# The sum of row and output bias: from GpSimd's queue to a late place in VectorE's

## The chip, the cores and the metric

One core of a Trainium2 chip runs the whole program in one launch. The metric is the device time of an execution in microseconds (us), as a median of several runs. One execution is also recorded by the hardware profiler; all rows below come from that one, and their times count from the start of its span.

## The reference

A row is one of 2048 tokens, 448 wide, bf16. Four blocks follow each other: a spectral block, an FFN, and the same two again, with the same weights each time.

```
x = x + A(layernorm(x))     # A: 2-D real FFT, times (w_r + i w_i), inverse FFT
x = x + B(layernorm(x))     # B: relu(x @ w1 + b1)^2 @ w2 + b2, inner width 1792
x = x + A(layernorm(x))
x = x + B(layernorm(x))
```

The layer norm has no gain and no bias. The change touches only the FFN's residual: `x + b2` is needed when the result of the second matrix product is added.

## The kernel before, in words

The 2048 rows lie in `x_sb` as 16 row tiles t of 128 rows by 448. The FFTs are matrix products with constant matrices. The inverse transform ends in `stage_TI(t)` and `stage_AI(t)`, for two row tiles at a time ("a pair"): TensorE multiplies, ScalarE copies the first product out of PSUM, TensorE multiplies again, and VectorE adds the second product into `x_sb`. That add is the first VectorE instruction of the FFN for that pair (form `x_sb<-ps,x_sb 128x896`).

Then the pair's layer norm. `ln_B1(t)` makes the statistics (L548 and L549 on VectorE, a square root on ScalarE) and the sum of the change: `xb = x_sb + b2row`, 128x896, on GpSimd. `ln_B2(t)` makes the reciprocal (L556) and `nmr` (L559) on VectorE, then normalizes the even tile on ScalarE and the odd tile on VectorE (L485) into `y2`; GpSimd copies a pad of 64 columns for each of the two (L480), and SyncE issues a transposing DMA into `yT`.

The FFN runs in four chunks of four row tiles. `h_part(c, fb)` is four matmuls of 512 columns, a Relu out of PSUM on ScalarE and a square on VectorE into `hbuf`, 14 times for each chunk. `o_tile(t)` is 14 matmuls of 448 columns, and VectorE adds `xb[:, t]` to their sum and writes `x_sb` again. `xb` lies in the same arena as the inverse transform's input Z, so it can be written only when Z has been read. After the first FFN, `second_A(t)` starts the next spectral block row tile by row tile; after the second, the row tile is stored.

The order of the instructions on each engine is worked out by a planner ahead of the launch, which simulates the engines with assumed costs. A unit is one instruction, or all matmuls into one PSUM tile. Its priority is the longest path to the end plus a bias that is set by hand; in the FFN the bias falls by 5500 for each row tile. Each engine takes, among the units whose inputs are there, the one that can start first, and the priority decides between equals:

```
            u.prio = tail + sum(op.cost for op in u.ops) + u.ops[-1].lat
            u.prio += u.bias
                    start = max(r, free[e])
                    key = (start, -u.prio, u.seq)
```

On the chip, each engine then runs its list strictly in that order, and waits on semaphores for what the other engines and the DMAs bring. The assumed cost of the sum is set in the helper `tt`: `rate = 0.96 if isinstance(a, _PsAP) or eng == "pool" else 1.92`, and `cost=_free(o) / rate + 65.0` nanoseconds. All operations recorded by `tt` carry line L476, all matmuls L454, all ScalarE operations L472.

Of the kernel before, what the change touches and what calls it, by code (L numbers as in the profile page):

```python
# [6 lines left out]
ALU = mybir.AluOpType  # L7
# [3 lines left out]
P = 128  # L11
S = 2048
D = 448
# [141 lines left out]
def _res(a):  # L155
    return a.ap() if isinstance(a, _PsAP) else a
# [210 lines left out]
def _free(ap):  # L367
    n = 1
    for step, cnt in list(ap.ap)[1:]:
        n *= cnt  # L370
    return n


def bass_interleave_layers__spectral_gfnet__dense_activation_squared_relu__prompt_kernel(nc, A_x, A_w_r, A_w_i, B_x, B_w1, B_b1, B_w2, B_b2, out):
# [4 lines left out]
    sch = _Sched()  # L379

    with ExitStack() as es:
        onchip = set()

        def sb(name, shape, dt=BF16):
            t = es.enter_context(nc.sbuf_tensor(name, shape, dt))
            onchip.add(t.name)
            return t

        x_sb = sb("x_sb", [P, NT, D])
# [6 lines left out]
        xb = arena[:, 2 * FB * 512:2 * FB * 512 + NT * D].rearrange("p (t d) -> p t d", t=NT)  # L396
# [23 lines left out]
        b2row = sb("b2row", [P, D])  # L420
# [53 lines left out]
        def tt(o, a, b, op, eng="dve"):  # L474
            rate = 0.96 if isinstance(a, _PsAP) or eng == "pool" else 1.92
            sch.add(eng, lambda e: e.tensor_tensor(o, _res(a), b, op), [a, b], [o], cost=_free(o) / rate + 65.0)  # L476
# [69 lines left out]
        def ln_stats(ts_):  # L546
            for t in ts_:
                small(lambda e, t=t: e.bn_stats(st[:, t, 0:6], x_sb[:, t, :]), [x_sb[:, t, :]], [st[:, t, 0:6]], 530.0)  # L548
                small(lambda e, t=t: e.bn_aggr(mv[:, t, 0:2], st[:, t, 0:6]), [st[:, t, 0:6]], [mv[:, t, 0:2]])  # L549
            a, b = ts_[0], ts_[-1] + 1  # L550
            act(rstd[:, a:b, 0], mv[:, a:b, 1], ACT.Sqrt, bias=epst[:, 0:1])
# [158 lines left out]

        def ln_B1(t):
            ln_stats([t, t + 1])
            tt(xb[:, t:t + 2, :], x_sb[:, t:t + 2, :], b2row[:, None, :].to_broadcast([P, 2, D]), ALU.add, eng="pool")

        def ln_B2(t):
            ln_rstd([t, t + 1], True)
# [48 lines left out]
        def ffn(last):  # L765
            for t in range(0, NT, 2):
                sch.bias = 5500.0 * (NT - t)
                stage_TI(t)
                stage_AI(t)
                ln_B1(t)  # L770
                ln_B2(t)
            for c in range(4):
                sch.bias = 22000.0 * (4 - c)
                for fb in range(FB):
                    h_part(c, fb)
                for t in range(4 * c, 4 * c + 4):
                    sch.bias = 5500.0 * (NT - t)
                    o_tile(t)
                    if last:
                        dma("sp", out_dram[:, t, :], x_sb[:, t, :])  # L780
                    else:
                        ln_stats([t])
                        ln_rstd([t], False)
                        second_A(t)
# [90 lines left out]
```

## Time and profile before

| | |
|---|---|
| time, median of 3 runs | 338.5 us (338.15 to 339.89) |
| the profiled execution | 338.62 us, span 336.8 us |
| TensorE clock, mean granted | 0.965 of full |
| busy share of the span: PE, DVE, ACT, POOL | 85%, 61%, 53%, 17% |

PE is TensorE, PEld its weight load, DVE is VectorE, ACT is ScalarE, POOL is GpSimd. [...] The span begins with the first instruction and ends with the last; the remaining 1.8 us of the execution lie around it. In a row of the chain of waits, the time is that for which the chain stayed with this instruction; in a row of the timeline it is the instruction's own duration, and what stands in square brackets is how long its engine had been idle, and what ended that.

### The profile page before, as it was taken

The numbers are of one execution on the slowest core, as the hardware profiler recorded it, in microseconds if no ns is written. First come the engines' busy times: TensorE is split into PE (matmuls) and PEld (weight loads), VectorE is DVE, ScalarE is ACT, GpSimd is POOL, SyncE is SP. The second block draws the span as 40 slices with busy tenths as digits, with TensorE's granted clock in tenths as the row PEclk, the third lists the DMA queues.
The fourth block names the chain that finished last, engine by engine and source line by source line (L and its number), as shares of the span: only waits on it lengthen the run. The fifth ranks groups of instructions, "written<-read, shape, count | busy, mean of one in ns | idle before, by whom it ended". The sixth has DMA issues, their size and how long they took to land.

```text
span 336.8 us, 4428 instructions
## 1 busy us (share of the span) xinstructions
PE 285.0 (85%) x1574; PEld 154.8 (46%) x1574; DVE 205.1 (61%) x499; ACT 178.5 (53%) x293; POOL 56.3 (17%) x81
## 2 busy tenths in 40 slices
PE   0979857857799999899996975774799999999996
PEld 0656534533354454455454652443344445445442
DVE  5705992799867555776455499159973342463432
ACT  2669955655634706645813885555573271451730
POOL 4991000454300000200000000045530000010000
PEclk9999977999999999999999898799789999999999
DMA  7994000033210000010000000002231100002001
GB/s 300 409 371 75 1 2 0 0 69 70 50 34 0 0 2 0 0 34 1 0 2 0 0 2 0 0 0 65 63 79 31 41 0 29 27 0 74 14 14 41
DMA packets 25621, 16.00 MB, mean 48 GB/s; under 512 B 19392, under 2 KB 24000, under 8 KB 25600
## 3 DMA queue, kind: packets, MB, share of 16 engines
q1 hardware_dynamic: 25312, 15.43, 15.0%
q10 hardware_dynamic: 288, 0.30, 0.3%
q8 instruction: 12, 0.20, 0.2%
q14 instruction: 9, 0.07, 0.1%
HBM read 9.70 MB, written 1.84 MB: 34 GB/s over the span
## 4 chain that ended last, share of the span: by engine, by line
PE 64%; DVE 24%; ACT 5%; issue 2%; POOL 2%; DMA 1%; DVEq 0%; POOLq 0%; ACTq 0%
PE ps L454 64%; DVE tmp L476 7%; DVE x_sb L476 4%; DVE st L548 4%; DVE arena L476 3%; DVE tmp L485 2%; ACT arena L472 2%; DVE nmr L559 2%; ACT XA L472 2%; DMA x_sb<-in_A_x_dram 1%; ACT VT L472 1%; POOL Fs L485 1%; DVE mv L549 1%; POOL Ms L485 1%; DVE rstd L556 0%
## 5 line engine op out<-in xcount | busy, mean ns | idle before, releaser
L454 PE MATMUL ps<-yT,W_sb 128*128 128x512 bf16 x448 | 101.7, 387 | 5.6 <-ACT arena L472 5.6
L472 ACT ACTIVATE arena<-ps,b1f 128x512 bf16<-128x512 f32 x112 | 75.3, 685 | 47.0 <-PE ps L454 47.0
L454 PE MATMUL ps<-W_sb,arena 128*128 128x448 bf16 x448 | 86.9, 352 | 0.0
L476 DVE TENSOR_TENSOR arena<-arena 128x512 bf16<-128x512 bf16 x112 | 49.6, 443 | 40.0 <-ACT arena L472 39.9
L454 PEld LDWEIGHTS ps<-yT,W_sb 128*128 128x128 bf16 x448 | 44.2, 99 | 61.2 <-ACT arena L472 8.1
L476 POOL TENSOR_TENSOR arena<-x_sb,b2row 128x896 bf16<-128x896 bf16 x16 | 30.3, 1907 | 215.7 <-DVE x_sb L476 179.5
L454 PEld LDWEIGHTS ps<-W_sb,arena 128*128 128x128 bf16 x448 | 43.8, 98 | 40.1
L472 ACT ACTIVATE XA<-ps 128x512 bf16<-128x512 f32 (+1 forms) x48 | 32.5, 701 | 28.1 <-PE ps L454 27.7
L476 DVE TENSOR_TENSOR x_sb<-ps,arena 128x448 bf16<-128x448 f32 x32 | 19.9, 623 | 37.0 <-PE ps L454 37.0
L548 DVE BATCH_NORM_STATS2 st<-x_sb 128x6 f32<-128x448 bf16 x64 | 38.4, 614 | 3.0 <-DMA x_sb<-in_A_x_dram 2.4
L454 PE MATMUL ps<-H_sb,arena 128*128 128x256 bf16 x128 | 22.9, 330 | 11.3 <-DVE arena L476 9.9
L472 ACT ACTIVATE arena<-ps 128x904 bf16<-128x904 f32 x32 | 28.0, 931 | 5.9 <-PE ps L454 5.6
L472 ACT ACTIVATE rstd<-mv,epst 128x2 f32<-128x2 f32 (+1 forms) x40 | 11.7, 293 | 35.5 <-DVE mv L549 35.4
L476 DVE TENSOR_TENSOR x_sb<-ps,x_sb 128x896 bf16<-128x896 f32 x16 | 16.8, 1071 | 18.6 <-PE ps L454 18.6
L472 ACT ACTIVATE VT<-ps 128x512 bf16<-128x512 f32 (+1 forms) x36 | 18.6, 551 | 13.9 <-PE ps L454 13.6
L454 PEld LDWEIGHTS ps<-H_sb,arena 128*128 128x128 bf16 x128 | 13.5, 115 | 20.5 <-DVE arena L476 14.3
L454 PE MATMUL ps<-XA,FI_sb 128*128 128x448 bf16 x64 | 14.1, 354 | 9.5 <-ACT XA L472 9.5
L485 DVE TENSOR_SCALAR tmp<-x_sb,mv,rstd 128x224 bf16<-128x224 bf16 (+1 forms) x48 | 20.3, 453 | 1.4
L472 ACT ACTIVATE tmp<-x_sb,nmr,rstd 128x448 bf16<-128x448 bf16 x16 | 12.2, 759 | 13.1 <-DVE nmr L559 12.9
L476 DVE TENSOR_TENSOR tmp<-arena 128x904 bf16<-128x904 bf16 (+1 forms) x16 | 8.9, 567 | 16.2 <-ACT arena L472 16.1
L454 PE MATMUL ps<-Fs,x_sb 128*128 128x256 bf16 x32 | 9.8, 324 | 10.0 <-POOL Fs L485 9.1
L454 PE MATMUL ps<-arena,G_sb 128*128 128x452 bf16 (+1 forms) x72 | 15.1, 342 | 3.3 <-ACT arena L472 2.0
(40 smaller groups left out, 208.3 us busy)
## 6 DMA issues: line engine op xcount, KB each, us to landing
x_sb<-in_A_x_dram SPq DMA_DIRECT2D x4, 448.0 KB, 5.3
out_dram<-x_sb SPq DMA_DIRECT2D x16, 112.0 KB, 1.7
W_sb<-in_B_w_dram SPq DMA_DIRECT2D x1, 1568.0 KB, 19.7
W_sb<-in_B_w_dram SPq DMA_DIRECT2D x1, 1344.0 KB, 15.1
yT<-in_A_w_r_dram SPq DMA_DIRECT2D x1, 900.0 KB, 9.1
yT<-in_A_w_i_dram SPq DMA_DIRECT2D x1, 900.0 KB, 10.9
H_sb<-c_H SPq DMA_DIRECT2D x1, 896.0 KB, 12.1
G_sb<-c_G SPq DMA_DIRECT2D x1, 672.0 KB, 7.4
```

Source lines behind the costliest of these rows:

```text
L454: sch.add("pe", lambda e: e.matmul(_res(o), lhsT, rhs, start=start, stop=stop, skip_group_check=skip), [lhsT, rhs], [o], cost=max(_free(rh ...
L472: sch.add("act", lambda e: e.activation(o, _res(i), func, **kw), rd, [o], cost=c)
L476: sch.add(eng, lambda e: e.tensor_tensor(o, _res(a), b, op), [a, b], [o], cost=_free(o) / rate + 65.0)
L485: sch.add(eng, lambda e: e.tensor_scalar(o, i, s1, s2, op0=op0, **kw), rd, [o], cost=_free(o) / (1.4 if eng == "pool" else 1.92) + 65.0)
L548: small(lambda e, t=t: e.bn_stats(st[:, t, 0:6], x_sb[:, t, :]), [x_sb[:, t, :]], [st[:, t, 0:6]], 530.0)
L549: small(lambda e, t=t: e.bn_aggr(mv[:, t, 0:2], st[:, t, 0:6]), [st[:, t, 0:6]], [mv[:, t, 0:2]])
L559: small(lambda e: e.scalar_tensor_tensor(out=n, in0=m, scalar=-1.0, in1=r, op0=ALU.mult, op1=ALU.mult), [m, r], [n])
```

## The change

The sum is no longer put in GpSimd's queue but in VectorE's, with the planner's bias lowered by 30000 for this one unit, and nothing else is edited.

```
 
         def ln_B1(t):
             ln_stats([t, t + 1])
-            tt(xb[:, t:t + 2, :], x_sb[:, t:t + 2, :], b2row[:, None, :].to_broadcast([P, 2, D]), ALU.add, eng="pool")
+            sch.bias -= 30000.0
+            tt(xb[:, t:t + 2, :], x_sb[:, t:t + 2, :], b2row[:, None, :].to_broadcast([P, 2, D]), ALU.add)
+            sch.bias += 30000.0
 
         def ln_B2(t):
```

## Rows read from the trace of the kernel before

**Rows 1.** Busy time by stage: PE, PEld, DVE, ACT, POOL, then PEclk, DMA share, GB/s

```profile
60.90:75.50 14.60, 9.63 (x72) 6.32 (x71) 14.60 (x32) 7.95 (x13) 8.58 (x8) 1.00 0.16 36
75.50:90.20 14.70, 11.11 (x50) 4.36 (x47) 14.56 (x31) 8.78 (x17) 6.60 (x6) 1.00 0.24 55
222.50:236.80 14.30, 9.43 (x65) 5.92 (x63) 14.24 (x31) 6.69 (x11) 8.82 (x8) 0.97 0.17 38
236.80:241.90 5.10, 3.14 (x10) 1.02 (x9) 5.10 (x11) 2.60 (x5) 3.48 (x3) 0.76 0.24 54
241.90:255.70 13.80, 13.80 (x57) 5.91 (x58) 10.03 (x30) 11.30 (x19) 2.86 (x4) 0.88 0.34 76
```

**Rows 2.** Chain that ended last, first FFN's layer norms: start, us, what

```profile
60.86 2.09 DVE x_sb L476 x2
...
65.41 0.38 DVE nmr L559
...
67.82 1.31 DVE nmr L559
...
79.55 1.84 DVE nmr L559
...
84.89 2.35 DVE arena L476 x2
...
88.17 0.09 DVE nmr L559
...
90.24 49.56 PE ps L454 x250
```

**Rows 3.** Timeline of GpSimd, first FFN's layer norms

```profile
62.04 3.72 POOL L476 TENSOR_TENSOR arena<-x_sb,b2row 128x896 bf16<-128x896 bf16 x2 [32.97 <-PE ps L454]
...
67.24 1.88 POOL L476 TENSOR_TENSOR arena<-x_sb,b2row 128x896 bf16<-128x896 bf16 x1 [0.30 <-DVE rstd L556]
69.99 0.29 POOL L480 COPY tmp<-tmp 128x128 bf16<-128x128 bf16 x1 [0.88 <-DVE st L548]
...
84.97 1.99 POOL L476 TENSOR_TENSOR arena<-x_sb,b2row 128x896 bf16<-128x896 bf16 x1 [2.43 <-DVE x_sb L476]
```

**Rows 4.** Chain that ended last, second FFN's layer norms

```profile
226.96 0.51 DVE nmr L559
...
230.50 0.39 DVE nmr L559
230.89 1.95 DVE tmp L485
...
234.76 0.31 DVE tmp L485
...
237.79 0.38 DVE nmr L559
238.18 1.95 DVE tmp L485
...
241.90 91.62 PE ps L454 x444
```

**Rows 5.** Timeline of GpSimd, last pair of the first FFN and second FFN

```profile
139.77 1.90 POOL L476 TENSOR_TENSOR arena<-x_sb,b2row 128x896 bf16<-128x896 bf16 x1 [47.60 <-DVE x_sb L476]
...
228.99 3.71 POOL L476 TENSOR_TENSOR arena<-x_sb,b2row 128x896 bf16<-128x896 bf16 x2 [0.37 <-DVE x_sb L476]
...
236.28 3.71 POOL L476 TENSOR_TENSOR arena<-x_sb,b2row 128x896 bf16<-128x896 bf16 x2 [0.37 <-DVE x_sb L476]
```

**Rows 6.** Timeline of all engines around the first FFN's last pair

```profile
139.60 2.63 DVE L485 TENSOR_SCALAR tmp<-x_sb,mv,rstd 128x224 bf16<-128x224 bf16 x4
...
141.79 1.00 PE L454 MATMUL ps<-FA_sb,tmp 128*128 128x256 bf16 x7 [1.52 <-DVE tmp L485]
...
142.69 1.06 DVE L485 TENSOR_SCALAR tmp<-x_sb,mv,rstd 128x224 bf16<-128x224 bf16 x4
```

**Rows 7.** Groups of VectorE instructions by form: busy us, mean ns of one

```profile
L476 DVE TENSOR_TENSOR arena<-arena 128x512 bf16<-128x512 bf16 x112 | 49.6, 443 | 40.0 <-ACT arena L472 39.9
...
L476 DVE TENSOR_TENSOR x_sb<-ps,x_sb 128x896 bf16<-128x896 f32 x16 | 16.8, 1071 | 18.6 <-PE ps L454 18.6
L476 DVE TENSOR_TENSOR tmp<-tmp,Wt 128x904 bf16<-128x904 bf16 x24 | 13.8, 624 | 0.1
```

## The prediction

> **What bounds the kernel now.** I read the busy time by stage first, since the change touches only the stages in which the layer norms of the two FFNs are made. Two stretches stand out: 60.9 to 90.2 and 222.5 to 241.9 us. In both, VectorE is busy for practically the whole time, TensorE is not [rows 1]. In the first, TensorE works 9.63 + 11.11 = 20.7 of 29.3 us, so it is idle for 8.6; in the second 9.43 + 3.14 = 12.6 of 19.4, idle for 6.8. Behind each stretch TensorE is the chain: 49.6 us in one piece from 90.24, 91.6 us in one piece from 241.90 [rows 2, 4]. So in these two stretches VectorE sets the end, and only time that it gives back there, or elsewhere where TensorE waits for it, is worth anything. A shorter queue on GpSimd by itself is worth nothing.
>
> Next I read the chain of waits inside these stretches, instruction by instruction, and looked for VectorE instructions that are much longer than others of their form. There are many. `nmr` works on two numbers per partition and takes 0.09 us at 88.17, but 1.31 at 67.82 and 1.84 at 79.55 [rows 2]. The 448-wide normalization takes 0.31 us at 234.76, but 1.95 at 230.89 and at 238.18 [rows 4]. Two squares at 84.89 take 2.35 us together, where the mean of one is 0.443 [rows 2, 7].
>
> Then I laid GpSimd's timeline beside it. The long `nmr` of 67.82 ends at 67.82 + 1.31 = 69.13; GpSimd's sum began at 67.24 and ends at 67.24 + 1.88 = 69.12 [rows 2, 3]. The `nmr` of 65.41 ends at 65.79; the two sums of 62.04 end at 65.76. The two squares end at 87.24; the sum of 84.97 ends at 86.96, which leaves 0.28 for the second square. In the second FFN the two sums of 228.99 last 3.71 us together, so the first ends near 230.85 and the second at 232.70: the `nmr` of 230.50 ends at 230.89, and the normalization behind it at 232.84 [rows 4, 5]. The pair of 236.28 repeats this: 238.13 and 239.99 against 238.17 and 240.13. The squares aside, these six ends agree within 0.15 us, and three kinds of VectorE instruction show it. I read it so: while GpSimd makes the sum, a VectorE instruction of these kinds waits until the sum is finished, and VectorE's whole queue stands behind it.
>
> [...]
>
> **What the change removes.** In the first FFN's stretch: 0.38 - 0.09 = 0.29 at 65.41; 1.31 - 0.09 = 1.22 at 67.82, and two more of the same size a round of 4.0 us apart, 3.7 in all; 1.84 - 0.09 = 1.75 at 79.55; and 2.35 - 2 x 0.443 = 1.46 for the squares [rows 2, 7]. Sum 7.2 us. In the second FFN's: 0.51 - 0.09 = 0.42, 0.30, 1.95 - 0.31 = 1.64, 0.29 and 1.64 [rows 2, 4], sum 4.3 us. Outside the two stretches there is one more place. The first FFN's last pair comes late, and its sum runs from 139.77 for 1.90 us [rows 5]. Four normalizations of 224 columns take 2.63 us there and 1.06 just after, so 1.57 are a wait, and TensorE stands idle for 1.52 until they are done, in the middle of its solid stretch [rows 6]. That is 1.5 us. GpSimd's own 16 sums of about 1.9 us leave its queue; what is left there are the pad copies of 0.29, which wait for the normalized row already now [rows 3], so the shorter queue itself is counted at nothing.
>
> **What it adds.** Sixteen VectorE additions of 128x896 bf16, both inputs in SBUF. This form isn't in the trace. The nearest row is the product of 128x904 with both inputs in SBUF, 0.624 us [rows 7]; from the other side, the same width read from PSUM in f32 takes 1.071 us. I take 0.6: type, memory and width are those of the first row, and a bias row that is read twice is still read element after element. At the other end I keep 1.0.
>
> [...]
>
> **Where the additions land.** The bias of -30000 is worth 30000 / 5500 = 5.5 row tiles, and the layer norm's path to the end is longer than the sum's by some thousands on top, so the sum of pair t gives way to the norms of pairs up to t + 6 and goes ahead of pair t + 8. That is so only while VectorE always has something ready; where the planner sees a gap, the sum goes in at once, since the earliest start comes before the priority. All that the planner decides ahead of the first sum is unchanged: the sum isn't on the longest path, so no earlier priority moves, and up to 60.86 us I expect the same trace. In the first stretch six pairs are normed before TensorE runs solidly. By the rule three additions lie ahead of that (pairs 0, 2, 4); at worst seven do. In the second, the rule puts two ahead, at worst six. The rest goes into the product stretches. There, VectorE is busy 10.03 of 13.80 us even at the start [rows 1], so it has room for 0.6 now and then. If that cover were gone, a square would be late by 0.6 and, at a chunk's end, the second product with it.
>
> Nothing is queued behind a new wait on VectorE: the addition needs only the pair's `x_sb`, written earlier by VectorE itself, `b2row`, loaded at the start, and Z's last reader on TensorE, which is past when the first GpSimd sum starts at 62.04 [rows 3]. SyncE's queue issues what it issued before.
>
> **The sum.** First stretch: -7.2 + 3 x 0.6 = -5.4; with seven ahead -7.2 + 4.2 = -3.0. Not all of it can reach TensorE: of its 8.6 us of idle time 5.0 lie before 75.5, waiting for the first normalized and transposed rows. I take -4.5. The single stall: -1.5. Second stretch: -4.3 + 2 x 0.6 = -3.1, with six ahead -0.7; I take -3.1, as TensorE has 6.8 us of idle time to give. Together -9.1: the profiled execution's 338.62 becomes 329.5. It lies 0.1 above the median of the runs, so the same figure holds for the median.
>
> TensorE's clock is left out of this sum. It falls from 0.97 to 0.76 of full behind the lull of the second stretch and is at 0.88 over the next 13.8 us [rows 1]; at full clock those 13.8 us would be 13.8 x 0.88 = 12.1. A shorter lull may spare this 1.7, an equal one keeps it.
>
> **Rivals.**
> - *The additions eat what the lock gives back.* More of them sit ahead of TensorE's solid stretch than the rule says (all seven and six: -3.0 - 0.7 - 1.5 = -5.2, 333.4), or one costs 1.0, which makes -7.2 + 3.0, -4.3 + 2.0 and -1.5, together -8.0, 330.6. Both at once: -0.2 + 1.7 - 1.5, 338.6. For it speaks that the planner fills gaps; against it, that VectorE has hardly any there.
> - *The clock stays up.* The forecast and another 1.7, and with no addition ahead of the solid stretches up to 3.0 more: 325 to 328.
> - *Another wait is next.* The first product needs two pairs normalized, padded and transposed; if that path and ScalarE's queue set TensorE's start and VectorE was only busy beside it, little but the single stall is gained: 336. Against it: the chain runs through VectorE nearly without a break.
> - *The long instructions aren't GpSimd's doing* (the other side). Then all stalls stay, and VectorE gets 3 to 7 additions in the first stretch and 2 to 6 in the second: 5 to 13 x 0.6, +3.0 to +7.8, middle 344. It decides if a long `nmr` or normalization is seen with GpSimd idle. Against it stand the six ends that agree. [...]
> - *The planner doesn't do as it says*, and puts all additions so early that they precede the norms: that is the first rival's worst.
>
> **How the numbers follow.** Forecast 0.68, additions eat it 0.12, clock 0.08, another wait 0.06, not GpSimd's 0.06. Two kernels of this length can be told apart from 0.5%, 1.7 us. Faster by more: the first three but for 0.02 of the second, and half of the fourth: 0.88; within: 0.06; slower: 0.06. The forecast's own range is 325 to 333. The range reaches down to the clock's case, 324, since every stall removed without an addition ahead would give -7.2 - 1.5 - 4.3 - 1.7 = -14.7, and up to 335.5, two us over the additions' first case.
>
> **What would show it.** Right: no `nmr` over 0.2 us and no 448-wide normalization over 0.5; rounds of a pair in the first stretch of 3 us instead of 4; TensorE solid from about 86 instead of 90.2, no idle time of 1.5 near 136 (where 140 was), and 3 us less in the second stretch; additions of 0.6 us. Wrong: long VectorE instructions that end with no GpSimd instruction; additions of 1 us; TensorE waiting for the transposed rows with VectorE idle; or squares that wait behind additions.

## The result, and the profile after

The changed kernel takes 325.95 us (median of 4 runs, 324.58 to 326.29), against 338.32 us before (4 runs): a ratio of 0.9618, 95% interval 0.9577 to 0.9659, 12.4 us less. The ratio and its interval, here and below, leave out executions in which a kernel ran clearly slower than its own fastest, so they are not quotients of the medians. The forecast was 329.5 with a range of 324.0 to 335.5. The profiled execution takes 326.29 us, with a span of 324.5 us and a mean granted clock of 0.968.

The forms of VectorE's instructions come first (busy us, mean ns of one | idle before):

```profile
L476 DVE TENSOR_TENSOR arena<-x_sb,b2row 128x896 bf16<-128x896 bf16 x16 | 9.7, 617 | 0.0
...
L485 DVE TENSOR_SCALAR tmp<-x_sb,mv,rstd 128x448 bf16<-128x448 bf16 x16 | 6.3, 392 | 0.0
...
L559 DVE SCALAR_TENSOR_TENSOR nmr<-mv,rstd 128x2 f32<-128x2 f32 x16 | 2.5, 154 | 0.3
```

The addition costs 0.617 us, beside the 0.624 of the product that it was measured by [rows 7]. `nmr` is at 0.154 us in the mean and the normalization at 0.392, and none reaches 0.2 or 0.45: all the long ones of [rows 2] and [rows 4] are gone.

The chain that ended last, in the first of the two layer-norm stretches (start, us, what; the view ends at 100 us, and TensorE's last piece goes on behind it):

```profile
60.76 2.09 DVE x_sb L476 x2
...
67.46 0.06 DVE nmr L559
...
70.22 0.06 DVE nmr L559
...
71.34 0.57 DVE arena L476
71.91 1.00 DVE x_sb L476
72.91 0.09 DVE rstd L556
73.00 0.06 issue
73.06 3.61 PE ps L454 x16
76.67 0.04 issue
76.72 23.29 PE ps L454 x114
```

A round of a pair without an addition now takes 2.76 us (67.46 to 70.22), where it was 4.0. The first addition stands at 71.34, right ahead of the fifth pair's add from PSUM: the sum of pair 0 gives way to the norms of pairs 2 and 4 and the statistics of pair 6 and goes ahead of pair 8, about where the bias puts it. And TensorE's solid stretch starts at 73.06, not at 90.24. The first chunk's product needs only the first two pairs in both kernels; before, it began at 75.57, but stopped three times up to 90.24, for 1.49, 0.24 and 1.88 us. Now it doesn't stop, and the later pairs' norms run beside it. The other hole of before, the 1.52 us that TensorE stood idle at the first FFN's last pair [rows 6], is gone as well; no idle time stands in the row of the same matmuls:

```profile
131.48 3.14 PE L454 MATMUL ps<-FA_sb,tmp 128*128 128x256 bf16 x24
```

The busy time over each whole FFN, from its first add out of PSUM to the start of its last (the columns are those of [rows 1]). Before:

```profile
60.86:179.83 118.97, 108.85 (x582) 55.67 (x581) 85.81 (x210) 61.34 (x107) 17.66 (x16) 1.00 0.08 19
222.56:333.55 110.99, 104.12 (x516) 50.70 (x514) 59.45 (x135) 49.83 (x77) 17.33 (x16) 0.97 0.13 35
```

After:

```profile
60.76:171.66 110.90, 108.45 (x582) 55.86 (x581) 80.22 (x219) 61.84 (x107) 3.40 (x8) 1.00 0.09 20
216.98:321.02 104.04, 100.76 (x516) 49.54 (x514) 57.87 (x143) 49.53 (x78) 3.40 (x8) 1.00 0.15 38
```

The first number is the length, the second TensorE's busy time. The first FFN is 8.1 us shorter: TensorE's idle time fell from 118.97 - 108.85 = 10.1 to 2.5 us. The second is 6.9 us shorter: the idle time fell from 6.9 to 3.3, and TensorE's busy time from 104.1 to 100.8 for the same matmuls, since the granted clock no longer falls there. It is 1.00 of full, where it was 0.97, 0.76 and 0.88 in the stretches of [rows 1]; TensorE was busy for 9.04 of 12.29 us before its solid stretch, against 9.43 of 14.30 and 3.14 of 5.10 then:

```profile
216.98:229.27 12.29, 9.04 (x65) 5.62 (x63) 12.29 (x34) 7.55 (x14) 0.88 (x3) 1.00 0.24 53
229.27:245.00 15.73, 15.73 (x74) 7.01 (x75) 15.73 (x46) 13.43 (x23) 2.23 (x4) 1.00 0.27 61
```

The two FFNs give 15.0 us. The second spectral block between them takes some of it back: from 179.83 to 222.56 it was 42.7 us, from 171.66 to 216.98 it is 45.3, so 2.6 us longer. Up to 60.8 us nothing moved. 15.0 - 2.6 is the 12.4 of the result.

### The profile page after: what moved, and what is told of

Same layout as the page of the kernel before. It is cut to its first block, busy times and chain, and to the rows that moved or that the text cites. A ratio compares the mean times of both kernels' runs of the same rounds, so it can differ in the third digit from the quotient of the medians.

```text
span 324.5 us, 4410 instructions
## 1 busy us (share of the span) xinstructions
PE 281.5 (87%) x1574; PEld 154.1 (47%) x1574; DVE 198.6 (61%) x515; ACT 178.4 (55%) x293; POOL 28.2 (9%) x65
## 4 chain that ended last, share of the span: by engine, by line
PE 71%; DVE 17%; ACT 5%; issue 2%; POOL 2%; DMA 1%; DVEq 0%; POOLq 0%; ACTq 0%
PE ps L454 71%; DVE tmp L476 7%; DVE x_sb L476 3%; DVE st L548 3%; ACT arena L472 3%; DVE arena L476 2%; ACT VT L472 1%; DMA x_sb<-in_A_x_dram 1%; POOL Fs L485 1%; ACT XA L472 1%; DVE tmp L485 1%; DVE mv L549 1%; POOL Ms L485 1%; POOL VT L480 0%; DVE rstd L556 0%
## 5 line engine op out<-in xcount | busy, mean ns | idle before, releaser
L454 PE MATMUL ps<-yT,W_sb 128*128 128x512 bf16 x448 | 98.2, 379 | 1.8 <-DVE nmr L559 1.6
L454 PEld LDWEIGHTS ps<-yT,W_sb 128*128 128x128 bf16 x448 | 43.4, 98 | 54.9 <-issue 2.4
L476 DVE TENSOR_TENSOR arena<-arena 128x512 bf16<-128x512 bf16 x112 | 47.0, 422 | 34.5 <-ACT arena L472 34.4
L480 POOL COPY tmp<-tmp 128x128 bf16<-128x128 bf16 x16 | 6.8, 424 | 257.3 <-ACT tmp L472 247.7
L472 ACT ACTIVATE rstd<-mv,epst 128x2 f32<-128x2 f32 (+1 forms) x40 | 11.7, 293 | 31.0 <-DVE mv L549 30.3
L454 PEld LDWEIGHTS ps<-H_sb,arena 128*128 128x128 bf16 x128 | 13.5, 114 | 21.1 <-DVE arena L476 15.6
L454 PE MATMUL ps<-TD_sb,XA 128*128 128x226 bf16 x128 | 16.6, 285 | 2.2 <-ACT XA L472 1.7
L454 PE MATMUL ps<-arena,G_sb 128*128 128x452 bf16 (+1 forms) x72 | 14.4, 337 | 4.7 <-ACT arena L472 3.7
L476 DVE TENSOR_TENSOR tmp<-tmp,Wt 128x904 bf16<-128x904 bf16 (+1 forms) x32 | 16.2, 565 | 0.2
## 6 DMA issues: line engine op xcount, KB each, us to landing
H_sb<-c_H SPq DMA_DIRECT2D x1, 896.0 KB, 12.4
```

The lines of the kernel that those rows point to most:

```text
L454: sch.add("pe", lambda e: e.matmul(_res(o), lhsT, rhs, start=start, stop=stop, skip_group_check=skip), [lhsT, rhs], [o], cost=max(_free(rh ...
L472: sch.add("act", lambda e: e.activation(o, _res(i), func, **kw), rd, [o], cost=c)
L480: sch.add(eng, lambda e: e.tensor_copy(o, _res(i)), [i], [o], cost=_free(o) / rate + 65.0)
```

## The experiments

The theory is that of the prediction: GpSimd's sum holds up VectorE instructions for as long as it lasts. The prediction and the expectations call this wait the lock; the runs show when it comes and how long it is, not what brings it about. The rival is that the engines' new order, which the planner works out afresh, made the gain. The stages below are taken from the timeline of VectorE, from the first add out of PSUM (`x_sb<-ps,x_sb`) of an FFN to the start of the last add of the residual (`x_sb<-ps,arena`), and the second spectral block from the latter to the former. The ratio given for each run is against the kernel before on the same chip. There the kernel before ran between 334.2 and 341.1 us, at mean granted clocks of 0.950 to 0.978, so the stages of the profiles say more than the last microsecond of a total.

**The sum cut short, the order of before.** Only the length of GpSimd's instruction differs from the kernel before; the output lacks most of the sum.

```
-            tt(xb[:, t:t + 2, :], x_sb[:, t:t + 2, :], b2row[:, None, :].to_broadcast([P, 2, D]), ALU.add, eng="pool")
+            o, a, b = xb[:, t:t + 2, :], x_sb[:, t:t + 2, :], b2row[:, None, :].to_broadcast([P, 2, D])
+            sch.add("pool", lambda e: e.tensor_tensor(o[:, :, 0:2], a[:, :, 0:2], b[:, :, 0:2], ALU.add), [a, b], [o],
+                    cost=_free(o) / 0.96 + 65.0)
```

> The kernel before with every engine's order kept; only GpSimd's sum is cut to two columns of each row tile (so most of the sum is left out of the output). If GpSimd's long sum holds VectorE up (theory), the 13.0 us of long instructions go without any new plan: no nmr above 0.3 us in the two layer-norm stretches, no 1.5 us hole in the first FFN's products, 325 to 330 us. If the gain came from the new plan of the engines (rival), nothing moves by more than 1.5 us: 337 to 340 us.

Measured: 325.37 us, ratio 0.9666 (0.9579 to 0.9752). The group of `nmr` in this run (ns min/median/max):

```profile
L559 DVE SCALAR_TENSOR_TENSOR nmr<-mv,rstd x16: 144/155/164, 65.5 to 290.5; 128x2 f32<-128x2 f32 x16
```

And its busy time over the two FFNs:

```profile
60.95:171.68 110.73, 108.28 (x582) 55.91 (x581) 76.89 (x210) 61.77 (x107) 4.30 (x16) 1.00 0.09 20
215.27:320.28 105.01, 100.92 (x516) 49.70 (x514) 54.46 (x136) 49.71 (x77) 4.05 (x16) 1.00 0.17 37
```

No `nmr` is above 0.164 us, both FFNs are about as short as in the changed kernel, and no instruction has a new place. The rival fails as the sole cause. Cutting the sum also empties GpSimd's queue, but that is not what gave the time: in the kernel before, GpSimd had been idle for 0.27 us or more ahead of each of its 16 pad copies, until the normalized row was there, so none of them stood behind a sum.

**The new order, the sum back on GpSimd.** The plan is that of the changed kernel; after it is made, the 16 sums are moved into GpSimd's list at the moment at which VectorE was to do them.

```
         sch.schedule()
+        for op in [op for op in sch.ops["dve"] if op.moved]:
+            sch.ops["dve"].remove(op)
+            op.eng = "pool"
+            i = sum(1 for q in sch.ops["pool"] if q.pos > op.pos)
+            sch.ops["pool"].insert(len(sch.ops["pool"]) - i, op)
```

> The changed kernel with its planned order on every engine, the sums alone taken out of VectorE's list and put into GpSimd's at the same planned moments. Theory: the long VectorE instructions are back, each ending with a GpSimd sum; in the first layer-norm stretch at least two sums lie beside VectorE work, and the time goes back to between 332 and 341 us. Rival (the plan gave the gain): 324 to 327 us, VectorE's 16 additions of 0.6 us even spared.

Measured: 330.83 us, ratio 0.9842 (0.9746 to 0.9939). Neither number was hit: it lies 1.2 us below the theory's and 3.8 above the rival's. The late place helps GpSimd's sums too, since fewer of them meet VectorE's norms:

```profile
71.74 1.88 POOL L478 TENSOR_TENSOR arena<-x_sb,b2row 128x896 bf16<-128x896 bf16 x1
74.75 1.88 POOL L478 TENSOR_TENSOR arena<-x_sb,b2row 128x896 bf16<-128x896 bf16 x1
...
85.70 5.92 POOL L478 TENSOR_TENSOR arena<-x_sb,b2row 128x896 bf16<-128x896 bf16 x3
```

The first starts at 71.74 instead of 62.04 [rows 3]. Most of them meet squares instead, and hold them up: a square takes 0.572 us in the mean here, against 0.422 in the changed kernel, so the long VectorE instructions did come back, in a place where they cost less.

```profile
L478 DVE TENSOR_TENSOR arena<-arena 128x512 bf16<-128x512 bf16 x112 | 63.5, 572 | 33.7 <-ACT arena L474 33.3
```

**The order of before, the sum on VectorE.** The same exchange from the kernel before, in the other direction (`"pool"` and `"dve"` swapped in the lines above), so the additions stand early.

> The kernel before with its planned order, the sums alone taken out of GpSimd's list and put into VectorE's at the same planned moments, so early. Theory: 13.0 us of waiting go, six or seven additions of 0.57 us come in ahead of TensorE's solid work in each FFN, 6.8 to 8 us: 326 to 333 us, with no long nmr. Rival (the plan gave the gain, the lock is nothing): 338 to 344 us.

Measured: 332.7 us, ratio 0.9871 (0.9744 to 0.9997). The theory's range holds it, at its upper end, and no `nmr` is above 0.2 us.

**What VectorE's additions still cost.** The changed kernel, its order kept, with the addition cut to two columns of each row tile; most of the sum is missing from the output.

```
+            o, a, b = xb[:, t:t + 2, :], x_sb[:, t:t + 2, :], b2row[:, None, :].to_broadcast([P, 2, D])
+            sch.add("dve", lambda e: e.tensor_tensor(o[:, :, 0:2], a[:, :, 0:2], b[:, :, 0:2], ALU.add), [a, b], [o],
+                    cost=_free(o) / 1.92 + 65.0)
```

> The changed kernel with every order kept, and VectorE's addition cut to two columns of each row tile (so most of the sum is left out of the output): what the additions still cost. One addition of 0.57 us stands ahead of TensorE's solid stretch in each FFN, the rest lies beside products: 0.5 to 1.5 us less than the changed kernel, about 325. If the additions delay squares and with them TensorE, 3 us or more less.

Measured: 324.57 us, ratio 0.9601 (0.9555 to 0.9647), 1.4 us under the changed kernel's median; 0.7 of that lies in the FFNs, where the additions are.

Together these give a small table, the sum of both FFNs in us, each from one profiled execution (a second one of the changed kernel gave the same 214.9):

| | early (order of before) | late (order of the changed kernel) |
|---|---|---|
| sum on GpSimd | 118.97 + 110.99 = 229.96 | 114.92 + 107.16 = 222.08 |
| sum on VectorE | 114.31 + 108.22 = 222.53 | 110.90 + 104.04 = 214.94 |
| sum cut short | 110.73 + 105.01 = 215.74 | 110.32 + 103.91 = 214.23 |

A sum on GpSimd costs the FFNs 229.96 - 215.74 = 14.2 us early and 7.9 late; on VectorE 6.8 early and 0.7 late. Of the 14.2, 3.8 are TensorE's busy time for the same matmuls, nearly all of it in the second FFN, where the granted clock was 0.97 of full, against 1.00 with the sum cut short. The order by itself, with no sum to speak of, is worth 1.5.

**GpSimd's sums with nobody waiting for them.** The changed kernel, and besides it the same 16 sums on GpSimd into a spare buffer.

```
             ln_stats([t, t + 1])
+            tt(spare[:], x_sb[:, t:t + 2, :], b2row[:, None, :].to_broadcast([P, 2, D]), ALU.add, eng="pool")
             sch.bias -= 30000.0
```

> The changed kernel with, besides, the same 16 sums on GpSimd into a spare buffer that nobody reads, as long as those of the kernel before. The plan of the other engines is not tied to them. Theory: they hold up VectorE again, 1 to 1.7 us each where they meet its work: 330 to 342 us. Rival (GpSimd's sums cost only through what waits for their result): 324 to 327.5 us.

Measured: 339.69 us, ratio 1.0116 (0.9991 to 1.0241), 13.7 us over the changed kernel. The FFNs take 119.5 and 110.3 us, as long as before, and no instruction reads what the sums write. TensorE and ScalarE have the order of the changed kernel, and of VectorE's instructions only a few small ones and additions stand elsewhere, all in the second FFN. `nmr` is long again, 0.879 us in the mean against 0.154:

```profile
L560 DVE SCALAR_TENSOR_TENSOR nmr<-mv,rstd 128x2 f32<-128x2 f32 x16 | 14.1, 879 | 0.3
```

So it is their running that costs.

**GpSimd instructions that only write.** The same place, with a memset as long as the sum.

```
             ln_stats([t, t + 1])
+            sch.add("pool", lambda e: e.memset(spare[:], 0.0), [x_sb[:, t:t + 2, :]], [spare[:]], cost=998.0)
             sch.bias -= 30000.0
```

> The changed kernel with, besides, 16 GpSimd instructions that wait for the same rows but only write: a memset of 2304 columns into a spare buffer, about 1.9 us each. If any GpSimd instruction holds VectorE up, nmr, squares and normalizations are long again and the time goes to 335 to 341 us, as with the idle sums. If only one that reads SBUF holds up instructions with two SBUF inputs, nmr and squares stay short and only the normalizations (one input) may be long: 325 to 333 us.

Measured: 337.69 us, ratio 1.0002 (0.9966 to 1.0037). VectorE's forms in this run:

```profile
L477 DVE TENSOR_TENSOR arena<-arena 128x512 bf16<-128x512 bf16 x112 | 46.7, 421 | 34.1 <-ACT arena L473 33.9
...
L486 DVE TENSOR_SCALAR tmp<-x_sb,mv,rstd 128x448 bf16<-128x448 bf16 x16 | 19.8, 1238 | 0.0
...
L560 DVE SCALAR_TENSOR_TENSOR nmr<-mv,rstd 128x2 f32<-128x2 f32 x16 | 2.4, 152 | 0.3
```

One of the memsets on GpSimd's timeline, and one of the normalizations on VectorE's:

```profile
67.62 2.02 POOL L714 MEMSET spare<- 128x2304 bf16 x1 [0.69 <-DVE x_sb L477]
```

```profile
68.14 0.14 DVE L560 SCALAR_TENSOR_TENSOR nmr<-mv,rstd 128x2 f32<-128x2 f32 x1
68.20 1.57 DVE L486 TENSOR_SCALAR tmp<-x_sb,mv,rstd 128x448 bf16<-128x448 bf16 x1
```

While the memset runs (to 69.64), `nmr` with its two inputs in SBUF passes in 0.14 us, and the normalization with one tensor input waits to 69.77. The squares stay at 0.421. So in these runs it depends on what both instructions do which one is held: beside the sum, which reads and writes, both kinds are long (`nmr` 0.879 us in the mean above, the normalization 1.95 us against 0.31 in [rows 4]); beside the memset, which only writes, the normalization is (1.238 us in the mean) and `nmr` is not (0.152). The kinds were foreseen, the time was not: 16 normalizations of 1.238 - 0.392 = 0.85 us more each are 13.5 us, and the run is 11.7 us longer than the changed kernel, above the 333 that I allowed for this case.

**The changed kernel without the lowered bias.** The sum is VectorE's but keeps its pair's priority.

```
-            sch.bias -= 30000.0
             tt(xb[:, t:t + 2, :], x_sb[:, t:t + 2, :], b2row[:, None, :].to_broadcast([P, 2, D]), ALU.add)
-            sch.bias += 30000.0
```

> The changed kernel without the lowered bias: the sum is VectorE's, but keeps its pair's own priority. Theory: the lock is gone all the same, but more additions of 0.57 us stand ahead of TensorE's solid stretch, four to seven in each FFN instead of one to two: 2 to 6 us over the changed kernel, 328 to 332. If the late place is worth nothing, 325 to 327.

Measured: 334.75 us, ratio 0.9863 (0.9786 to 0.9941): slower than the changed kernel, but not for the reason that I gave. The second FFN takes 105.0 us, 1.0 more than in the changed kernel, and TensorE's solid stretch of the first starts 12.2 us after the first add out of PSUM, where it was 12.3, although three additions lie ahead of it. The loss is in the middle of the first FFN, in the timeline of TensorE:

```profile
150.15 1.04 PE L454 MATMUL ps<-FA_sb,tmp 128*128 128x256 bf16 x8 [1.21 <-DVE tmp L485]
155.37 15.18 PE L454 MATMUL ps<-yT,W_sb 128*128 128x512 bf16 x56 [4.18 <-issue]
```

and of SyncE's queue:

```profile
152.54 1.23 SPq L444 DMA_TRANSPOSE yT<-tmp  x1
```

The last pair's normalized rows are transposed at 152.54, and the last chunk's first product starts only at 155.37: the plan has put the last pair's norm so late that TensorE waits 4.18 us. Behind it the granted clock is at 0.90 of full from 156.00 to 182.29, where it was 1.00 from 73.48 to 140.00, and the 56 matmuls of that chunk take 15.18 us, where those of the second chunk take 12.25. That hole, and the low clock behind it, belong to this plan. This run therefore doesn't price the bias by itself; the table above does.

**The second spectral block put back into its old order.** The changed kernel, with the units of that block tied to the order of the kernel before on TensorE, ScalarE and VectorE; all other orders come out as in the changed kernel.

```
+        for line in self.fixed:
+            us = [self.units[i] for i in line]
+            for u, v in zip(us, us[1:]):
+                if v not in order[u]:
+                    order[u].add(v)
+                    npred[v].add(u)
         free = {e: 0.0 for e in self.ENGINES}
```

> The changed kernel with one thing put back: inside the second spectral block every engine takes its units in the order of the kernel before (the order of the rest is untouched). If the 2.6 us that this block lost come from the new order, they return: 323 to 324 us. If they come from TensorE's granted clock after the first FFN (0.64 in the block's first 9 us against 0.80 before), the time stays within 1 us of the changed kernel, 325 to 326.5. Half of each: 324.5 to 325.

Measured: 324.3 us, ratio 0.9601 (0.955 to 0.9652). To compare it with the changed kernel on one chip, both were run once more:

> The changed kernel itself, on the same chip as the next one, so that the two can be compared: 324.5 to 326.5 us.

> The changed kernel with the second spectral block in the order of the kernel before, on the same chip as the changed kernel. If the order of that block costs what the stages say (43.0 us against 45.3, part of it the clock), it is 0.8 to 2.3 us faster than the changed kernel here; if the difference was the chip or the clock, within 0.5 us.

Measured there: 326.0 us (324.88 to 326.83, ratio 0.9597, 0.9554 to 0.964) for the changed kernel and 323.94 us (323.91 to 324.29, ratio 0.9544, 0.9505 to 0.9583) with the old order in the block. The ranges don't touch; the old order is 2.1 us better, and this version is the best of all that were run. Not all of the 2.1 is the order, though. Over the block, the changed kernel and this version stood so in their profiled executions:

```profile
172.76:216.91 44.15, 29.67 (x202) 19.71 (x201) 24.83 (x58) 26.78 (x40) 0.00 (x0) 0.88 0.00 0
171.97:214.72 42.75, 30.55 (x202) 19.24 (x200) 24.11 (x59) 26.88 (x40) 0.00 (x0) 0.88 0.00 0
```

At the same mean granted clock of 0.88 the old order is 1.4 us shorter. Another 0.8 lies ahead of the first FFN, whose first add out of PSUM is at 61.87 and at 61.07, although the two programs are alike up to there. The clock has a part as well. In the first run of the changed kernel, the block's first stretch, up to the end of the matmuls that open it, stood so:

```profile
171.66:180.69 9.03, 6.17 (x32) 3.93 (x30) 2.18 (x6) 3.34 (x6) 0.00 (x0) 0.64 0.00 0
```

and in the kernel before:

```profile
179.83:187.80 7.97, 5.15 (x33) 3.73 (x32) 2.19 (x6) 3.34 (x5) 0.00 (x0) 0.80 0.00 0
```

The same 32 matmuls (the second window takes in one more) take 6.2 us at a mean granted clock of 0.64 (1.00 up to 174.00, 0.57 up to 176.00 and 0.50 from there on), and 5.2 at 0.80 (1.00 up to 184.00, 0.66 up to 186.00 and 0.50 from there on). In both windows TensorE stands idle for 2.13 us behind its first matmuls, before the clock falls.

## Why the prediction was right, point by point

**The mechanism** was right. GpSimd's sum holds VectorE up while it runs: shown by the sum cut short, which gives the whole gain in the old order (325.37 us), and by the idle sums, which take it all back (339.69 us). One thing is finer than the prediction had it: `nmr`, which has two inputs in SBUF, takes 0.879 us in the mean beside the idle sums and 0.152 beside the memsets, where the normalization, which has one tensor input, takes 1.238. What makes this difference was not shown.

**The waits and the additions** are told apart by TensorE's time, since the forecast was made of what TensorE would wait less: 6.0 us in the first FFN and 3.1 in the second, 9.1 in all. Its idle time fell by 7.7 and 3.6, together 11.3, so this sum was 2.2 short. Two steps failed. The first is "In the first stretch six pairs are normed before TensorE runs solidly". That was itself a consequence of the stalls: ScalarE's copies and Relus waited behind normalizations that waited for `nmr`, and TensorE waited behind ScalarE. In the kernel before, on ScalarE and on TensorE:

```profile
73.18 0.76 ACT L472 ACTIVATE tmp<-x_sb,nmr,rstd 128x448 bf16<-128x448 bf16 x1 [2.60 <-DVE nmr L559]
...
88.28 0.76 ACT L472 ACTIVATE tmp<-x_sb,nmr,rstd 128x448 bf16<-128x448 bf16 x1 [2.44 <-DVE nmr L559]
```

```profile
74.80 0.93 PE L454 MATMUL ps<-XA,FI_sb 128*128 128x448 bf16 x4 [1.87 <-ACT XA L472]
...
90.24 3.63 PE L454 MATMUL ps<-yT,W_sb 128*128 128x512 bf16 x16 [1.88 <-ACT arena L472]
```

With the stalls gone, TensorE runs on from the first chunk's two pairs, and the norms and additions of the other pairs lie beside its products. So not five additions of 0.6 stand ahead of the solid stretches, but one in each: -7.2 + 0.6 = -6.6 and -4.3 + 0.6 = -3.7 where -5.4 and -3.1 were taken, and all 16 together cost 0.7 us where 3.0 were taken. Their price was right: 0.6 against 0.617.

The second is the step from -5.4 to -4.5, for which 5.0 us of TensorE's idle time were read as "waiting for the first normalized and transposed rows". They were not. In that time TensorE stood between matmuls of the inverse transform, as at 74.80 above, and the product behind them, at 75.57, began without any idle time. Half of the 5.0 was the stalls again: the idle time of TensorE fell from 5.0 to 2.4 us ahead of the first product, and from 3.6 to nothing in the stretch behind it, together 6.1, near the -6.6.

**The clock** is the larger miss. TensorE's busy time for the same matmuls fell by 0.4 us in the first FFN and by 3.4 in the second, 3.8 in all. The 3.4 is the clock's, which was 0.97 of full over the second FFN before and is 1.00 now. The 0.4 isn't, since the granted clock was 1.00 over the first FFN both times, and its cause stays open. The prediction had named the clock, left it out of the sum as the less likely case and priced it at 1.7, from 241.9 to 255.7 us alone.

**The block between** was not thought of: up to 60.86 us the plan was rightly said to be unchanged, but nothing was said of what comes behind. The planner works from its simulated times, and a changed cost in the first FFN moved the order of the second spectral block. Of the 2.6 us, the order is worth 1.4, measured at the same granted clock. The other 1.2 is the clock's: over the block it was 0.85 in the changed kernel's first profiled execution, and 0.88 in the kernel before and in the second one.

So: -11.3 of TensorE's idle time, -3.8 of its busy time, +2.6 in the block between; together -12.5, where the medians differ by 12.4. The forecast had the first at -9.1 and lacked the other two, which partly cancel. That the time lies inside the range owes something to this luck: the version with the old order in the block ran in 323.94 us, just below the range's lower end of 324.

**The rivals.** Additions that eat the gain are real where they stand early, 6.8 us in the order of before, but not where the change puts them. That the clock stays up came true together with the forecast. That another wait is next, and that the stalls aren't GpSimd's, are refuted by the runs above. That the planner puts the additions early is refuted by the first one's place at 71.34. In the chances, the terms named for "faster by more" add up to 0.89, not 0.88.

## What to carry to other kernels

Before giving work to GpSimd to relieve VectorE, lay the two timelines side by side: a tiny VectorE instruction that ends with a long GpSimd one is the sign (here `nmr`, 0.879 us in the mean beside GpSimd's sums and 0.154 without them), and the price is what waits behind it, here 14 us for 30 us of GpSimd work that seemed free. Where the same work fits on VectorE at a third of the duration (here 0.617 us against 1.9 [rows 3]), put it there, and late: its place was worth as much as its engine (in the table, 7.9 us for the late place on GpSimd, 7.4 for VectorE in the early one). And when a planner makes the order, compare the order of the stages that the edit did not touch, because an edit elsewhere can move their order, here at a cost of 1.4 us.

## What the hardware did that was not expected

A GpSimd instruction is long beside VectorE's work too: in the changed kernel one pad copy in each FFN takes 1.34 us, where the other fourteen take 0.29. The one of the first FFN, with VectorE's rows beside it:

```profile
87.84 1.34 POOL L480 COPY tmp<-tmp 128x128 bf16<-128x128 bf16 x1 [4.04 <-ACT tmp L472]
```

```profile
87.54 1.15 DVE L476 TENSOR_TENSOR arena<-x_sb,b2row 128x896 bf16<-128x896 bf16 x2
88.61 0.42 DVE L476 TENSOR_TENSOR arena<-arena 128x512 bf16<-128x512 bf16 x1
```

The copy lasts from 87.84 to 89.18, across two additions and a square that follow each other without a gap and end at 88.69 and 89.03; the one of the second FFN, from 243.49 to 244.83, also lies across two additions and a square. I read it so that not one instruction held the copy but three in a row, but no run tests that. The first of the two copies is not on the chain that ended last, which is TensorE alone from 76.72 to 171.6.

The mean granted clock of one and the same program, the kernel before, lay between 0.950 and 0.978 from execution to execution, with 341 to 334 us to go with it. Of the stages, the second spectral block shows it most: with the same order it took 45.3, 44.2 and 42.5 us in three of the runs above (the changed kernel, its second run, and the new order with the sum on GpSimd), at mean granted clocks of 0.85, 0.88 and 0.92 over the block.
